# Layer 1, token tile 0: seven half-width products per pair of weight tiles, with a leaner attention start and a new instruction order

## The chip, the core and the metric

The kernel runs on one NeuronCore of a Trainium2 chip. Its engines are TensorE (PE in the profile; PEld is its weight load), VectorE (DVE), ScalarE (ACT), GpSimd (POOL) and SyncE (SP, which issues the loads here); 16 DMA engines move data. The metric is the device time of one execution in microseconds (us), as the median of several runs; lower is better.

## What is computed

Three stages follow each other: a linear attention with a decay per head, and two feed-forward layers, the first with ELU and the second with softplus between its two matrix products.

```python
def _attn_ref(q, k, v, lam):            # 2 x 8 heads x 768 tokens x 64
    ...
    for b in range(nb):                 # blocks of 64 tokens
        intra = np.einsum('bhic,bhjc->bhij', qb, kb) * Dmask[None]
        intra = np.einsum('bhij,bhjd->bhid', intra, vb)
        inter = np.einsum('bhid,bhde->bhie', qb * lam_pow[None], kv_state)
        out[:, :, sl] = intra + inter
        kv_state = lam_block[None, :, None, None] * kv_state + np.einsum('bhsd,bhse->bhde', kb_dec, vb)

x = attention, as 1536 tokens x 512
h = x @ w_in                            # 512 -> 2048
g = np.where(h > 0.0, h, np.exp(np.minimum(h, 0.0)) - 1.0)
x = g @ w_out                           # 2048 -> 512
h = x @ w_in2
g = np.maximum(h, 0.0) + np.log1p(np.exp(-np.abs(h)))
out = g @ w_out2
```

## The kernel before

**Number format.** Each large product is made of three matmuls in a rounded 32-bit format (`F32R`): a matrix is kept as a high part and a low part, and high x high, high x low and low x high are summed in PSUM (`product`, lines 335 to 337 for the first matrix of a layer; `m2_part`, line 386, for the second). Weights come from memory in 64-bit words, and four ScalarE and VectorE steps turn each tile of 128x512 into its two parts (lines 602 to 621 and the difference `minus`, line 527).

**Tiling.** The 1536 tokens are three tiles of 512 (tile 0, 1, 2). The 2048 inner features of a layer are 16 chunks of 128, in 8 pairs. Tile 0 is done plainly: one chunk takes 4 x 3 matmuls of 512 columns into one PSUM bank (`plain`, tile name `hps`). Tiles 1 and 2 together are done by a Strassen-Winograd scheme (`quick`): a pair of chunks for both tiles takes 7 products of 6 matmuls of 512 columns (tiles `pa`, `pb`, `pd`) in place of 8, with sums of weight tiles (`sum_ops`, tiles `s0`, `s1`, scratch `sumsw`) and sums of activations (`t1` to `t4`). Between the seven products ScalarE copies a bank out and VectorE adds to the copy, so that results share banks.

After a first product the activation function runs on ScalarE and VectorE (`act_ops`), which leaves the parts `g`; the second product then takes 12 matmuls for each chunk and tile into four banks `y`, and after several chunks VectorE adds those into `yacc` (line 1144). After layer 0, `split_ops` makes tile 0's new input parts out of `yacc`, and `second_sums` does so for tiles 1 and 2 with their sums.

**Attention.** The attention runs in 12 chunks of 128 tokens. `att_s` makes the scores (line 245), `att_sc` multiplies them by the decay mask on VectorE over 2 x 4 x 128 = 1024 columns (line 251), `att_x` makes the output (line 265), `att_state` the state's update (line 312, tile `stps`), `att_add` and `att_fade` keep the running state (lines 318 to 325), `att_prep` scales the queries by the decay powers `qpow` (line 222) and `att_prep_k` the keys (lines 228 and 230). `decays` fills the mask with 8 scans of 128 columns on VectorE, and `powers` fills `qpow` with 4 more.

**Order.** The program is written out by a planner in `build`: every step is an `Op` with a key (its due time), costs per engine (`MM3`, `SB_V` and others) and what it depends on, and `schedule` issues the ops engine by engine as its own clock says. `PLAN` lists the first products: `one` is a plain chunk of tile 0, `fast` a pair for tiles 1 and 2. In layer 1 four `one` are followed by two `fast`, four times. The order on every engine is then fixed. SP issues all loads, in the order of `FIRST_LOADS` first.

## Time and profile before

| | us |
|---|---|
| median of 3 runs | 556.19 (556.12 to 557.3) |
| the profiled execution | 555.85 |
| its span | 554.1 |
| first scores start on TensorE | 4.83 |
| last matmul starts | 549.90 |

The profiled execution's own time is 1.75 us more than its span and 0.34 us less than the median. A line of the profile gives the source line, the engine, the operation, the tile written and the tiles read, the shape, how often, the busy time and the mean length of one in ns. A length is from an instruction's start to its end; where instructions of one engine follow each other without a gap, the next starts before the last has ended, so the distance between two starts (called pitch here) is shorter than the length.

### The profile page before, as it was taken

Reading aid. Unit: us, or ns where it says so; the run is one execution under the profiler, and the core shown is the slowest. Engines: PE = TensorE matmul, PEld = TensorE weight load, DVE = VectorE, ACT = ScalarE, POOL = GpSimd, SP = SyncE. Lnnn points to the kernel's source line nnn. Section 1 sums busy time; section 2 is a strip of 40 time slices with the busy share of each in tenths; the row PEclk is TensorE's granted clock in tenths of the full one; section 3 lists DMA queues with packets and bytes.
Section 4 is the critical chain, followed back from the end, with each engine's and each line's share of the span. In section 5 each row is a group of like instructions: output and inputs, shape, how many; then the busy total and the mean of one; then the engine's idle time right before and its main releaser. Section 6 shows DMA issues by size and latency. Waiting matters only on the chain.

```text
span 554.1 us, 8536 instructions
## 1 busy us (share of the span) xinstructions
PE 541.4 (98%) x3215; PEld 447.4 (81%) x3215; DVE 492.4 (89%) x876; ACT 404.0 (73%) x758; POOL 2.2 (0%) x8
## 2 busy tenths in 40 slices
PE   7789999999999999999999999999999999999997
PEld 6677788888888888888888888888888888888885
DVE  7899999999489899657999999999999999986973
ACT  4677897768398487547877589979996779856820
POOL 0000000000000000000000000000000000000000
PEclk9999999999999999999999999999999999999999
DMA  8967443011024224201322101212231212000023
GB/s 325 397 227 272 155 152 112 2 38 55 23 77 151 77 76 148 81 1 38 103 71 94 38 1 38 77 38 77 76 101 52 77 39 76 1 0 2 1 99 129
DMA packets 14585, 49.84 MB, mean 90 GB/s; under 512 B 1744, under 2 KB 1744, under 8 KB 14544
## 3 DMA queue, kind: packets, MB, share of 16 engines
q1 hardware_dynamic: 14544, 49.30, 25.9%
q8 instruction: 25, 0.41, 0.3%
q14 instruction: 16, 0.13, 0.1%
HBM read 46.14 MB, written 3.15 MB: 89 GB/s over the span
## 4 chain that ended last, share of the span: by engine, by line
PE 90%; DMA 6%; DVE 1%; ACT 1%; SPq 0%; issue 0%; ACTq 0%
PE y L386 47%; PE pa L335 5%; PE pa L337 5%; PE pa L336 5%; PE hps L335 5%; PE hps L337 5%; PE hps L336 5%; DMA raw<-w 4%; PE pd L335 3%; PE pd L337 3%; PE pd L336 3%; DMA qk<-attqk 1%; PE pb L337 1%; PE pb L335 1%; PE pb L336 1%; DMA kv<-attkv 1%
## 5 line engine op out<-in xcount | busy, mean ns | idle before, releaser
L386 PE MATMUL y<-g,woh 128*128 128x512 f32 x384 | 118.4, 390 | 0.0
L386 PE MATMUL y<-woh,g 128*128 128x512 f32 x384 | 118.2, 389 | 0.0
L840 ACT ACTIVATE g<-v 128x512 fp32r<-128x512 f32 x96 | 60.3, 628 | 53.8 <-PE y L386 53.2
L527 DVE TENSOR_TENSOR g<-v,g 128x512 fp32r<-128x512 f32 x96 | 65.4, 685 | 21.4 <-ACT g L840 21.2
L386 PEld LDWEIGHTS y<-woh,g 128*128 128x128 f32 x384 | 72.1, 188 | 15.0
L386 PEld LDWEIGHTS y<-g,woh 128*128 128x128 f32 x384 | 71.9, 188 | 15.0 <-issue 0.2
L386 PE MATMUL y<-g,wol 128*128 128x512 f32 x192 | 74.7, 389 | 0.0
L386 PE MATMUL y<-wol,g 128*128 128x512 f32 x192 | 74.7, 389 | 0.0
L1144 DVE TENSOR_TENSOR yacc<-y,yacc 128x512 f32<-128x512 f32 x68 | 44.1, 684 | 7.2 <-PE y L386 7.2
L335 PE MATMUL hps<-xh,wih 128*128 128x512 f32 x128 | 50.3, 393 | 0.0
L336 PE MATMUL hps<-xl,wih 128*128 128x512 f32 x128 | 49.8, 389 | 0.0
L337 PE MATMUL hps<-xh,wil 128*128 128x512 f32 x128 | 49.8, 389 | 0.0
L602 ACT ACTIVATE r<-raw 128x512 f32<-128x512 f32 x64 | 42.6, 665 | 8.7 <-DMA raw<-w 4.1
L616 DVE CUSTOM_DVE_ANT_0 r<-r,c 128x1024 uint16<-128x1024 uint16 x64 | 43.8, 684 | 2.9 <-ACT c L606 2.5
L606 ACT ACTIVATE c<-raw 128x512 uint32<-128x512 uint32 x64 | 42.4, 662 | 0.7 <-DVE r L616 0.7
L386 PEld LDWEIGHTS y<-g,wol 128*128 128x128 f32 x192 | 36.0, 188 | 7.6
L386 PEld LDWEIGHTS y<-wol,g 128*128 128x128 f32 x192 | 36.0, 188 | 7.4
L821 DVE SCALAR_TENSOR_TENSOR u<-u,e 128x512 f32<-128x512 f32 x48 | 32.7, 683 | 3.2 <-ACT v L817 3.2
L527 DVE TENSOR_TENSOR v<-v,u 128x512 f32<-128x512 f32 x48 | 32.7, 684 | 0.2
L396 ACT ACTIVATE v<-v 128x512 f32<-128x512 f32 x48 | 29.9, 625 | 0.6
L396 ACT ACTIVATE e<-e 128x512 f32<-128x512 f32 x48 | 30.0, 625 | 0.4
L812 ACT ACTIVATE u<-e 128x512 f32<-128x512 f32 x48 | 29.8, 621 | 0.2
(174 smaller groups left out, 1084.6 us busy)
## 6 DMA issues: line engine op xcount, KB each, us to landing
raw<-w SPq DMA_DIRECT2D x64, 512.0 KB, 3.7
qk<-attqk SPq DMA_DIRECT2D x8, 512.0 KB, 7.2
kv<-attkv SPq DMA_DIRECT2D x8, 512.0 KB, 5.9
out<-yacc SPq DMA_DIRECT2D x12, 256.0 KB, 2.1
early<-attqk SPq DMA_DIRECT2D x2, 512.0 KB, 10.0
early<-attkv SPq DMA_DIRECT2D x2, 512.0 KB, 10.1
earlykv<-attkv SPq DMA_DIRECT2D x2, 512.0 KB, 11.2
earlyqk<-attqk SPq DMA_DIRECT2D x2, 512.0 KB, 10.4
```

The lines of the kernel that those rows point to most:

```text
L335: T.matmul(ps, wh[:, wo[i]], xa[i], start=(start and i == 0), stop=False, skip_group_check=True)
L336: T.matmul(ps, wh[:, wo[i]], xb[i], start=False, stop=False, skip_group_check=True)
L337: T.matmul(ps, wl[:, wo[i]], xa[i], start=False, stop=(stop and i == n - 1), skip_group_check=True)
L386: T.matmul(yps[m], a, b, start=(begins(key) and i == 0), stop=(ends(key) and i == 2))
L396: A.activation(out=o, in_=a, func=AF.Exp, scale=-1.0)
L527: engines[e].tensor_tensor(out=o, in0=a, in1=b, op=ALU.subtract)
L602: A.activation(out=r, in_=high.bitcast(F32), func=AF.Prelu, scale=2.0 ** -112, alpha=-2.0 ** 32)
L606: A.activation(out=box["c"], in_=box["low"], func=AF.Copy, scale=2.0 ** -29)
L616: V.tensor_tensor(out=ri, in0=ri, in1=box["c"], op=ALU.add)
L821: V.scalar_tensor_tensor(out=u, in0=u, scalar=-1.0, in1=box["e"], op0=ALU.add, op1=ALU.subtract)
L840: A.activation(out=g[:, 0], in_=box["v"], func=AF.Copy)
L1144: V.tensor_tensor(out=y, in0=yps[m], in1=y, op=ALU.add)
```

## The change

1. **Layer 1, tile 0.** The first four chunks (pairs 0 and 1) stay plain. Pairs 2 to 7 are done by the seven-product scheme over the tile's two halves of 256 tokens (`slim`; banks `za`, `zb`, `zd`). It takes the weight sums that tiles 1 and 2 use anyhow (`made_sums`). `zero_sums` replaces `split_ops` and makes the activation sums `z1`, `z2`, `z4` and, in place of a part of the input, a third. The plain product is no longer cut in four for the layer's first chunk.
2. **Attention.** The scores are packed so that the mask multiply covers 768 columns; the mask takes 4 + 8 scans of 64 columns; `qpow` comes from 8 small matmuls (`powers`) and one ScalarE copy. In `att_x` the second pairs of heads are split in two matmuls, with a `T.drain()` ahead of the last group. Fades go to GpSimd but for the first of them, as does the first chunk's key scaling.
3. **Start.** The small table `lam_t` is loaded from ScalarE's queue, and the first load of queries and keys is cut in two.
4. **Order.** New planner constants, a table `NUDGE` that shifts the keys of 52 ops, four shared scratch tiles (`e0` to `e3`), 12 activation buffers in place of 9, and 3 weight slots in place of 6 late in layer 1, whose room the `z` tiles take.

```diff
+NUDGE = {
+    338: -0.7, 340: -0.4, 344: 0.2, 353: 0.0, 356: 0.9, 360: -5.0, 362: 1.4, 364: 3.1, 373: 0.3, 384: -4.1, 387:
...
+SECOND = [
+    ("one", (0, 1, 2, 3)), ("fast", (0, 1)), ("slim", (2,)), ("fast", (2, 3)), ("slim", (3, 4)), ("fast", (4, 5)),
+    ("slim", (5, 6)), ("fast", (6,)), ("slim", (7,)), ("fast", (7,)),
+]
+UNITS = {2: (2,), 3: (3, 4), 5: (5, 6, 7)}
...
-    for b in range(4):
-        p += [("one", 1, c) for c in range(4 * b, 4 * b + 4)]
-        p += [("fast", 1, q) for q in (2 * b, 2 * b + 1)]
+    for kind, qs in SECOND:
+        p += [(kind, 1, q) for q in qs]
...
-        return n if n < 8 else 2 + (n - 8) % 6
+        return n if n < 8 else 2 + (n - 8) % 6 if n < NF + 4 else 5 + (n - NF - 4) % 3
...
     def setup():
-        nc.sync.dma_start(out=lam_t, in_=lamc)
+        A.dma_start(out=lam_t, in_=lamc)
...
-    def powers():
+    def powers(ps):
         for p in range(NPAIR):
-            V.tensor_tensor_scan(
-                out=qpow[:, p, :], data0=lam_t[:, H + p:H + p + 1].to_broadcast([P, P]), data1=zero,
-                initial=1.0, op0=ALU.mult, op1=ALU.add,
-            )
+            for e in range(2):
+                w = lam_t[:, H + NPAIR + 2 * p + e:H + NPAIR + 2 * p + e + 1].to_broadcast([P, 64])
+                x = dmask[:, e, p % 2, 0:2] if p < 2 else dmask[:, e, p % 2, 0::2]
+                T.matmul(
+                    ps[64 * e:64 * e + 64, P * p:P * p + P].rearrange("q (a i) -> q a i", a=2), w, x,
+                    start=True, stop=True, skip_group_check=True)
+
+    def powers_out(ps):
+        A.activation(out=qpow.rearrange("q a i -> q (a i)"), in_=ps, func=AF.Copy)
...
-        nc.sync.dma_start(out=qk, in_=attqk[g])
+        if g:
+            nc.sync.dma_start(out=qk, in_=attqk[g])
+        else:
+            for c in (slice(0, HALF), slice(HALF, DM)):
+                nc.sync.dma_start(out=qk[:, :, c], in_=attqk[g].rearrange("p (a i) -> p a i", a=2)[:, :, c])
...
-        sc[g] = ap2.tile([P, 2, NPAIR, P], F32, tag="sc", name="sc")
+        sc[g] = ap2.tile([P, 2, 384], F32, tag="sc", name="sc")
         V.tensor_tensor(
-            out=sc[g], in0=sps[g].rearrange("p e (a i) -> p e a i", a=NPAIR), in1=dmask, op=ALU.mult)
+            out=sc[g], in0=sps[g][:, :, :384], in1=dmask.rearrange("q e j a i -> q e (j a i)"), op=ALU.mult)
...
         for p, e in heads[0]:
-            intra(p, e, rows[e], 0, 64)
-        for p, e in heads[0]:
-            intra(p, e, slice(0, P), 64, 64)
+            intra(p, e, rows[e], 0, first_half(p))
+        for p, e in heads[0] + heads[1]:
+            intra(p, e, slice(0, P), 64, second_half(p))
+        if between:
+            between()
+        T.drain()
         for p, e in heads[1]:
-            intra(p, e, slice(0, P), 0, P)
+            intra(p, e, rows[1 - e], 0, first_half(p))
...
+            self.key += NUDGE.get(self.n, 0.0)
...
+    SLIM = 0.72
-    PILE, HELD, QUEUE, PACK = 2.9, 7.9, 3, 0.8
+    PILE, HELD, QUEUE, PACK = 2.9, 3.9, 1, 0.8
-    F_ON = {"G": (0.62, True), "V": (0.415, True)}
+    F_ON = {"G": (0.62, True)}
...
+        def slim(p):
...
+            p1 = pe(0, "a", lambda: (*halves[fa], c0), lambda: x(0, one), True, [need(fa), first[0]], bank_free)
+            k1 = copy_op("a", keys[0], one, pos[3] - 1.0, [p1])
+            p2 = pe(1, "b", lambda: (*halves[fa], c1), lambda: x(1, one), True, [need(fa), first[1]], bank_free)
+            a11 = add_op(keys[0], one, "b", pos[4] - 1.0, [p2, k1], lambda: give_bank(box["b"]))
+            p5 = pe(2, "d", lambda: W(0, c0), lambda: xt(1), True, [s12, t[1]], bank_free)
+            k5 = copy_op("d", keys[1], two, pos[4] - 1.0, [p5])
+            p6 = pe(3, "a", lambda: W(0, c1), lambda: xt(2), False, [k1, s12, t[2]])
+            k2 = copy_op("a", keys[0], two, pos[5] - 1.0, [p6, k1])
+            p3 = pe(4, "d", lambda: W(1, c0), lambda: x(1, two), False, [k5, s34, first[2]])
+            a12 = add_op(keys[0], two, "d", pos[6] - 1.0, [p3, k2], lambda: give_bank(box["d"]))
+            p7 = pe(5, "a", lambda: W(1, c1), lambda: xt(3), False, [k2, s34, t[3]])
+            a22 = add_op(keys[1], two, "a", pos[6] - 1.0, [p7, k5])
+            p4 = pe(6, "a", lambda: (*halves[fb], c1), lambda: xt(4), False, [a22, need(fb), t[4]])
+            k4 = copy_op("a", keys[1], one, nom["m2", keys[1]] - 3.0, [p4, k5], lambda: give_bank(box["a"]))
...
+        def zero_sums():
...
+            f1 = sub(pos[2], yy(0, one), yy(0, two), yy(0, one), [k11, k12, closed[0]])
+            f3 = sub(pos[2], yy(0, two), yy(1, two), yy(0, two), [f1, k12, k22])
+            f2 = sub(pos[3], yy(1, two), yy(1, two), yy(0, one), [f1, f3])
+            f4 = sub(pos[6], yy(1, one), yy(1, one), yy(1, two), [f2, k21])
```

Over the whole program the counts of instructions go from 384 to 240 matmuls of 512 columns into `hps`, and from none to 252 of 256 columns into `za`, `zb` and `zd`.

How the instructions stand is shown at three places. The first is VectorE at the attention's first chunks, from the first masked scores (`sc`) on; `xl` is the low part of the output, `state` and `faded` the running state. Before:

```order
L251 TENSOR_TENSOR sc<-aps_104,dmask 128x1024
L190 SCALAR_TENSOR_TENSOR qpow<-lam_t,zero 128x128 x4
L303 TENSOR_TENSOR xl_223<-aps_104,xh_222 128x4x128
L318 COPY state<-stps 128x256
L251 TENSOR_TENSOR sc<-aps_108,dmask 128x1024
L325 TENSOR_TENSOR faded<-state,qpow 128x256
L222 TENSOR_TENSOR qk<-qk,qpow 128x512
L251 TENSOR_TENSOR sc<-aps_104,dmask 128x1024
```

After:

```order
L325 TENSOR_TENSOR sc<-aps_107,dmask 128x768
L380 TENSOR_TENSOR xl_247<-aps_107,xh_246 128x4x128
L325 TENSOR_TENSOR sc<-aps_111,dmask 128x768
L279 TENSOR_TENSOR qk<-qk,qpow 128x512
L325 TENSOR_TENSOR sc<-aps_107,dmask 128x768
L395 COPY state<-stps 128x256
L279 TENSOR_TENSOR qk<-qk,qpow 128x512
L402 TENSOR_TENSOR faded<-state,qpow 128x256
```

The four scans for `qpow` are gone, the masked scores are narrower, and the state's first copy stands behind the third masked scores.

The second place is TensorE late in layer 1, where the sixth of the seven products hands its bank to the last one. Before, in a `fast` pair (tiles 1 and 2), with second products `y` between the two:

```order
L335 MATMUL pa<-t3h,s1h 128x512
L336 MATMUL pa<-t3l,s1h 128x512
L337 MATMUL pa<-t3h,s1l 128x512
L386 MATMUL y_4996<-woh_4435,g_5062 128x512 x2
L386 MATMUL y_4996<-wol_4463,g_5062 128x512
L386 MATMUL y_5004<-woh_4435,g_5062 128x512 x2
L386 MATMUL y_5004<-wol_4463,g_5062 128x512
L335 MATMUL pa<-t4h,wih_4637 128x512
```

After, in the last `slim` pair (pair 7 of tile 0):

```order
L412 MATMUL za<-xh_3146,s1h 128x256
L413 MATMUL za<-xl_3147,s1h 128x256
L414 MATMUL za<-xh_3146,s1l 128x256
L412 MATMUL za<-z4h,wih_5379 128x256
L413 MATMUL za<-z4l,wih_5379 128x256
L414 MATMUL za<-z4h,wil_5400 128x256
```

There nothing stands between the two products of that pair; in the other five `slim` pairs 6 to 36 matmuls `y` do.

The third place is SP's queue at the start. Before:

```order
L151 DMA lam_t<-lamc 128x12
L207 DMA qk<-attqk 128x1024
L217 DMA kv<-attkv 128x1024
L207 DMA qk<-attqk 128x1024
L217 DMA kv<-attkv 128x1024
```

After:

```order
L264 DMA qk<-attqk 128x2x256 x2
L274 DMA kv<-attkv 128x1024
L261 DMA qk<-attqk 128x1024
L274 DMA kv<-attkv 128x1024
L261 DMA qk<-attqk 128x1024
```

The table's load has left this queue, and the first load stands in two halves.

## Rows read from the trace of the kernel before

**Rows 1.** The page: busy time and share by engine, VectorE by slices, chain by engine.

```profile
PE 541.4 (98%) x3215; PEld 447.4 (81%) x3215; DVE 492.4 (89%) x876; ACT 404.0 (73%) x758; POOL 2.2 (0%) x8
...
DVE  7899999999489899657999999999999999986973
...
PE 90%; DMA 6%; DVE 1%; ACT 1%; SPq 0%; issue 0%; ACTq 0%
```

**Rows 2.** Busy time by stretch: length, then each engine's busy us and count.

```profile
core 0: us, PE busy (x) PEld busy (x) DVE busy (x) ACT busy (x) POOL busy (x), PEclk, DMA share, GB/s
5.00:25.00 20.00, 14.71 (x424) 12.55 (x424) 16.80 (x31) 12.51 (x41) 0.00 (x0) 1.00 1.02 397
25.00:51.00 26.00, 23.54 (x476) 19.28 (x476) 25.12 (x43) 18.94 (x45) 1.25 (x2) 1.00 0.74 271
...
300.00:500.00 200.00, 200.00 (x884) 165.55 (x883) 196.12 (x347) 163.97 (x302) 0.00 (x0) 1.00 0.15 48
500.00:550.30 50.30, 50.29 (x222) 41.29 (x221) 33.79 (x53) 24.04 (x41) 0.00 (x0) 1.00 0.13 46
```

**Rows 3.** Timeline of TensorE at 316 us: start, length, line, tiles, count.

```profile
316.19 0.39 PE L335 MATMUL pa<-xh,wih 128*128 128x512 f32 x1
316.42 0.39 PE L336 MATMUL pa<-xl,wih 128*128 128x512 f32 x1
```

**Rows 4.** Weight-load groups (count, busy us, mean ns); timeline of 256-column matmuls at the start.

```profile
L335 PEld LDWEIGHTS pa<-xh,wih 128*128 128x128 f32 x32 | 6.0, 188 | 1.2
...
L165 PEld LDWEIGHTS aps<-zr 128*128 128x128 f32 x4 | 1.0, 332 | 0.0
...
3.63 0.41 PE L165 MATMUL aps<-zr 128*128 128x256 f32 x1
3.85 1.05 PE L168 MATMUL warm<-zr 128*128 128x256 f32 x3
```

**Rows 5.** Waits of TensorE up to 52 us: us in total, times, longest.

```profile
PE aps L245 <- DMA qk<-attqk: 1.6, 2, 1.4
...
PE aps L265 <- DVE sc L251: 1.4, 1, 1.4
PE aps L245 <- DVE xl L303: 1.1, 2, 0.7
...
PE aps L265 <- DVE qk L222: 1.1, 2, 0.8
PE aps L265 <- DVE early L222: 0.8, 1, 0.8
```

**Rows 6.** Timeline of VectorE at 26 us, for its pitch by width.

```profile
26.45 0.68 DVE L303 TENSOR_TENSOR xl<-aps,xh 128x512 fp32r<-128x512 f32 x1
27.05 1.21 DVE L251 TENSOR_TENSOR sc<-aps,dmask 128x1024 f32<-128x1024 f32 x1
28.18 0.68 DVE L222 TENSOR_TENSOR earlyqk<-earlyqk,qpow 128x512 f32<-128x512 f32 x1
```

**Rows 7.** Groups by line and shape: scans for the powers, fades on both engines.

```profile
L190 DVE TENSOR_TENSOR_SCAN qpow<-lam_t,zero 128x128 f32<-128x128 f32 x4 | 1.4, 400 | 0.0
...
L325 POOL TENSOR_TENSOR faded<-state,qpow 128x256 f32<-128x256 f32 x2 | 1.2, 623 | 47.7 <-DVE state L320 47.7
```

**Rows 8.** Timeline of SP's first two loads.

```profile
0.80 0.38 SPq L151 DMA_DIRECT2D lam_t<-lamc  x1
1.24 0.42 SPq L207 DMA_DIRECT2D qk<-attqk  x1
```

**Rows 9.** Groups of small attention matmuls: count, busy us, mean ns of one.

```profile
L265 PE MATMUL aps<-sc,early 128*64 128x128 f32 x16 | 1.2, 273 | 0.0
...
L312 PE MATMUL stps<-early 128*64 128x64 f32 x32 | 1.1, 222 | 0.0
```

**Rows 10.** Groups of 256 columns: a copy of ScalarE and an operation of VectorE from PSUM.

```profile
L303 DVE TENSOR_TENSOR xl2b<-aps,xh2b 128x256 fp32r<-128x256 f32 x4 | 1.7, 420 | 1.3 <-ACT x L299 1.3
...
L295 ACT ACTIVATE xh2b<-aps 128x256 fp32r<-128x256 f32 x4 | 1.5, 382 | 0.5 <-PE aps L265 0.5
```

More of the change, by code (lines that the diff above doesn't have):

```diff
@@ L161, in setup @@
             T.matmul(ps[:, :P], zero, zero, start=True, stop=True)
[L163 to L166 removed]
+        for n, times in ((256, 5), (384, 2)):
             for i in range(times):
@@ L353, in body @@
             queue.append((layer, 0, c))
+        elif kind == "slim":
+            queue += [(layer, 0, 2 * q + i) for q in UNITS.get(c, ()) for i in range(2)]
         elif c % 2:
@@ L757, in take_v, with take_temp, copied @@
             return k, new_v(k)
-        eu = [0, 1]
+        vbuf = {}
+        temps = list(range(4))
+        def take_temp():
+            k = temps.pop(0)
+            return k, late["tp"].tile([P, TT], F32, tag=f"e{k}", name=f"e{k}")
+        def copied(key, e, src):
+            vbuf[key] = take_v(key)
+            if e == "A":
+                A.activation(out=vbuf[key][1], in_=src, func=AF.Copy)
+            else:
+                V.tensor_copy(vbuf[key][1], src)
         m1_seq, m2_seq = [], []
@@ L829, in act_ops @@
                 gate = v_gate(key)
-                o = Op({"A": SCALAR}, k, s1, after + [closed[0]], lambda: eu and gate())
+                o = Op({"A": SCALAR}, k, s1, after + [closed[0]], lambda: len(temps) > 1 and (not bank or gate()))
                 o = Op({"A": SCALAR}, k, s2, [o])
                 o = Either(PLUS_ONE, k, s3, [o])
-                o4 = Op({"A": SCALAR}, k, s4, [o])
-                o5 = Op({"V": SB_V}, k, s5, [o4])
-                o6 = Either(SOFT, k, s6, [o5], end=lambda: eu.append(box["i"]))
@@ L1166, in unit_ops @@
                 ysplit[t] = mine
[L1168 to L1186 removed]
+        tz, zdone = {}, {}
@@ L1275, in build @@
             if kind == "one":
-                o = plain(layer, 0, c, layer == 1 and c == 0)
+                o = plain(layer, 0, c)
                 xuse[0] = [o]
                 keys_done.add((layer, 0, c))
+                if (layer, c) == (1, 3):
+                    last_part[0]()
+            elif kind == "slim":
+                slim(c)
+                keys_done.update((layer, 0, 2 * c + i) for i in range(2))
             else:
@@ L1294, in body @@
     NV = 9
+    vfree = set(range(NV))
     W_LO = {"V": SB_V}
```

432 lines of the change are left out of this document (290 added, 142 removed), and 5 rows, old and new, of the table NUDGE.

## Prediction

> **What bounds the kernel now.** I read the page first: TensorE is busy for 98% of the span and stands on 90% of the chain that ended last [rows 1]. Then the stretches: from 51 us to the end of the products TensorE leaves next to nothing idle, and all of its lost time lies ahead of that, 5.3 us between 5 and 25 us and 2.5 us between 25 and 51 us [rows 2]. So a saved matmul after 51 us is saved time, as long as TensorE's inputs keep up. That they do is no matter of course: between 300 and 500 us VectorE is busy for 196.1 of 200 us, and only after 500 us does it have room, 33.8 of 50.3 us [rows 2]. Late in the program TensorE and VectorE are nearly level. At the start TensorE waits for VectorE in four groups that add up to 4.4 us (masked scores, low parts, scaled queries twice) and for a load, 1.6 us [rows 5]; VectorE is busy for 25.1 of 26 us between 25 and 51 us, and the DMA engines are full between 5 and 25 us [rows 2].
>
> **Strassen on tile 0: matmuls.** Removed are 144 matmuls of 512 columns (12 chunks of 12), added 252 of 256 columns (6 pairs, 7 products, 6 each). A 512-column matmul follows the one before it after 0.227 us (316.19 to 316.42; the starts of one chunk give 0.2267) [rows 3]. [...] The removed work is 144 x 0.2267 = 32.6 us, the added 252 x 0.120 = 30.2 us: **2.4 us less**; in proportion 4.1 us less. [...]
>
> The weight load is what could spoil this. One lasts 188 ns in the steady stretch [rows 4], longer than 120 ns. [...] If the load ran at a pace of its own and didn't quicken with the array, 188 ns would be the bound: 252 x 0.188 = 47.4 us, 14.7 us more than what is removed. I give that little, and take 0.130 us as the upper end (it breaks even).
>
> **Strassen on tile 0: the other engines.** VectorE gets 18 additions of 256 columns (three per pair), four sums and four more low parts of 512 columns, and four more copies that ScalarE did. Its pitch is 0.60 us for 512 columns (26.45 to 27.05) [rows 6]; for 256 I take 0.335 us, from the length of 0.420 [rows 10] less the 0.08 us by which 0.68 exceeds 0.60. That is 18 x 0.335 + 12 x 0.60 = 13.2 us. The room from 300 us on is 3.9 + 16.5 = 20.4 us [rows 2], and TensorE takes back 2.4 of it, so 4.8 us stay: VectorE has to be busy for about 98% to the end. It was so for 200 us without TensorE waiting; that the room after 500 us can be used follows from the order of the work (the final run of second products shrinks from 135 to 102 matmuls, so first products stretch further into it). ScalarE gets 24 copies of 256 columns and four high parts, about 10 us, and has 36 us free in 300 to 500 us [rows 2]: nothing.
>
> **Waits inside the seven products.** A product now lasts 0.72 us, not 1.36. When ScalarE has copied out the fourth product's bank, the sixth may go, and only the fifth lies between unless second products do; so it is with the third product, the fourth and the fifth. The loop is the end of a matmul (0.39 - 0.23 = 0.16 us after its stream) [rows 3], a copy of 0.38 us [rows 10] and two hand-overs that I put at 0.08 us each: 0.70 against 0.72 us. It fits if ScalarE is idle; it is busy for 82% [rows 2], so some 0.2 us is lost. By the order three pairs (4, 6, 7) have no second product there, with two such hand-overs each: 6 x 0.2 = 1.2 us; some copies will find ScalarE free, so 1.0 us. In pair 7 nothing at all lies between the sixth and the last product, while VectorE adds: 0.16 + 0.42 [rows 10] + 0.16 = 0.74 us. Together **1.7 us more**; between 0 and 4, since each VectorE step may queue.
>
> **The start and the attention.** The loads go out 0.44 us earlier (0.80 against 1.24) [rows 8], and since the DMA engines are full then, all early landings move with them: 0.4 us less. [...] VectorE loses the scans for the powers (1.4 us) and fades (seven of eight on GpSimd, two were: five x 0.33) [rows 7], and 256 of 1024 columns of twelve masked scores: a pitch of 1.13 us (27.05 to 28.18) [rows 6] against 0.60 for 512 is about 1.04 ns a column, so 12 x 0.27 = 3.2 us. Its new small steps cost what the narrower mask scans save. Of 6.3 us I credit TensorE with 2.4 us, over half of the 4.4 us of waits [rows 5], as several of these will wait for a load or a copy instead; bounds 0 and 4.4. A fade on GpSimd takes 0.62 us [rows 7], off TensorE's path. [...]
>
> On TensorE each chunk now empties the array once: a small matmul lasts 222 ns where 32 of them take 1.1 us, 34 ns each [rows 9], so 0.19 us is exposed. Two groups of 64 columns in place of one of 128 save next to nothing (0.6 us for eight of 128 columns [rows 9]). 12 x 0.13 = 1.6 us, part of it where TensorE waits anyway: 1.0 us more; bounds 0 and 2.4. The attention's sum is -0.4 - 2.4 + 1.0 = **1.8 us less**, between 4.8 less and 2 more.
>
> **The sum.** 555.85 (the profiled execution, 554.1 in its span) - 2.4 + 1.7 - 1.8 = 553.35 us. The median of the runs is 0.34 us above the profiled one: 553.7 us. What 0.2% means, 1.1 us, is about what a measurement of this kernel tells from no change.
>
> **Rivals.**
> 1. *Nothing gets in the way.* [...] Chance 0.18.
> 2. *The seven products don't pay.* Either 256 columns take 0.130 us (0 and the 1.7 of waits), or they take 0.120 and the waits 4 us (-2.4 + 4 = 1.6): 555.85 + 1.7 - 1.8 + 0.34 = 556.1 us. For it: three pairs go from product to product without second products. Against it: VectorE and ScalarE keep up with such hand-overs now. Chance 0.16.
> 3. *VectorE becomes the bound of layer 1 (slower).* Place: from 300 us on. If the 16.5 us after 500 us can't be filled, because VectorE waits there for TensorE's last products as it does now, 13.2 us meet 3.9 us of room: 9.3 us late, 555.85 + 9.3 - 1.8 + 0.34 = 563.7 us. It decides from the point where VectorE idles more than the 4.8 us left. The attention's relief of VectorE and the longer run of first products speak against it, the 98% for it. Chance 0.10.
> 4. *The weight load bounds 256 columns (slower).* The 188 ns of a load set the pitch, +14.7 in place of -2.4: 553.7 + 17.1 = 570.8 us. Against it the start's 0.22 us with loads of 332 ns [rows 4]. [...] Chance 0.04 for both.
>
> **The numbers.** The forecast, 553.7 us, gets 0.52; its own spread is 551.5 to 555.0. Faster by over 1.1 us are the forecast and rival 1: 0.70. Within 1.1 us is rival 2: 0.16. Slower: rivals 3 and 4, 0.14. A range of 549.8 to 557.5 us leaves out rivals 3 and 4 and the best of rival 1, about 2 in 10.
>
> **What would show it.** Right: `za` matmuls 0.12 us apart; TensorE without gaps from about 48 us on but for some tenths at pairs 4, 6 and 7; VectorE at 97 to 99% from 300 to 520 us and idle for less than 6 us behind that; the first product of layer 0 starting 1 to 3 us earlier. Wrong: `za` 0.19 us apart (rival 4); TensorE waiting for `g` or for VectorE's additions by several us in layer 1 (rival 3); waits at the first scores as long as now, with the drains on top.

## The result, and the profile after

The changed kernel takes **559.19 us** (median of 6 runs, 558.01 to 560.16) against 556.12 us of the kernel before beside it: ratio 1.0056, 95% interval 1.0037 to 1.0075. It is slower by 3 us, where the prediction said 553.7 us, faster, and 557.5 us at the most. The profiled execution lies at the median (559.15 us, span 557.4 us).

The page after, its busy line and the chain's shares by engine, as in [rows 1]:

```profile
PE 543.0 (97%) x3435; PEld 453.2 (81%) x3435; DVE 502.5 (90%) x907; ACT 413.5 (74%) x775; POOL 7.8 (1%) x14
...
PE 87%; DVE 7%; ACT 2%; issue 1%; DMA 1%; SPq 0%; DVEq 0%; ACTq 0%
```

TensorE is busy 1.6 us longer although columns were saved, and "issue", time in which an engine waited for nothing that the profile shows, is on the chain. The stretches, columns as in [rows 2]:

```profile
5.00:25.00 20.00, 14.80 (x400) 12.66 (x404) 12.38 (x24) 9.99 (x31) 3.09 (x4) 0.95 1.02 404
25.00:51.00 26.00, 24.22 (x514) 19.94 (x508) 22.75 (x38) 19.11 (x48) 2.93 (x4) 0.97 0.67 235
300.00:500.00 200.00, 199.20 (x974) 168.18 (x973) 195.89 (x351) 164.45 (x307) 0.00 (x0) 1.00 0.16 51
500.00:553.50 53.50, 52.98 (x254) 44.37 (x252) 47.72 (x83) 37.53 (x67) 0.00 (x0) 1.00 0.14 52
```

From 300 us on it is nearly as forecast: VectorE is busy for 98% up to 500 us and for 89% behind that, and TensorE lacks only 1.3 us. The start is not: between 5 and 25 us VectorE is busy for 4.4 us less than before (12.38 against 16.80), and TensorE has gained nothing from it. The first product of layer 0 starts at 30.63 us (26.14 before), the 100th matmul of 512 columns at 75.29 us (72.12 before): **the start loses 3.2 us**. From the 1200th on to the last, layer 1 for the most part, it is 229.06 us against 228.66: **0.4 us more**.

What TensorE waits for from 5 us to the first product, in the kernel before and then in the changed one (us in total, times, longest):

```profile
PE aps L245 <- DMA qk<-attqk: 1.4, 1, 1.4
PE stps L312 <- ACT earlykv L228: 1.4, 1, 1.4
PE aps L265 <- DVE sc L251: 1.4, 1, 1.4
PE aps L265 <- DVE early L222: 0.8, 1, 0.8
PE aps L245 <- DVE xl L303: 0.4, 1, 0.4
```

```profile
PE stps L389 <- issue: 2.5, 1, 2.5
PE aps L308 <- DMA qk<-attqk: 1.8, 1, 1.8
PE aps L339 <- issue: 1.2, 1, 1.2
PE aps L339 <- DMA kv<-attkv: 0.3, 1, 0.3
PE aps L339 <- DVE state L395: 0.3, 1, 0.3
```

The waits for VectorE fell from 2.6 to 0.3 us. In their place stand 3.7 us of "issue". The longer of these stops, in TensorE's timeline (start, length, line, tiles, count of records, idle time ahead; a record is the trace's entry for one instruction), and the kernel before at the same place:

```profile
18.80 0.56 PE L389 MATMUL stps<-early 128*64 128x64 f32 x11
21.87 0.39 PE L389 MATMUL stps<-early 128*64 128x64 f32 x5 [2.51 <-issue]
22.18 0.96 PE L308 MATMUL aps<-early 64*64 64x128 f32 x32
```

```profile
18.73 0.34 PE L312 MATMUL stps<-earlykv 128*64 128x64 f32 x4
20.44 0.57 PE L312 MATMUL stps<-earlykv 128*64 128x64 f32 x12 [1.38 <-ACT earlykv L228]
```

The stop falls into the middle of a group, after 11 of 16 records: no tile and no engine is waited for there. In the kernel before the view names ScalarE, but its last scaling of that tile had ended at 19.66 us, 0.8 us ahead of 20.44. What arrives in these microseconds beside the data is a packet of instructions; that they are TensorE's is read from their count (27 packets in the whole trace for its 6926 records, one for each 256). The DMA view by queue of 19.2 to 20.4 us (packets, MB, share of 16 engines):

```profile
q1 hardware_dynamic: 125, 0.45, 94.8%
q8 instruction: 1, 0.02, 5.3%
```

After the stop, the granted clock is 0.50 for 3.4 us (length, busy us of PE, PEld, DVE, ACT, POOL, granted clock, DMA share, GB/s):

```profile
19.00:22.80 3.80, 1.29 (x43) 1.09 (x42) 1.83 (x3) 3.19 (x10) 1.00 (x1) 1.00 1.02 406
22.90:26.30 3.40, 3.40 (x69) 3.05 (x60) 3.10 (x5) 0.00 (x0) 0.73 (x1) 0.50 1.02 412
26.30:51.00 24.70, 22.92 (x487) 18.75 (x486) 21.45 (x37) 19.11 (x48) 2.63 (x3) 1.00 0.65 225
```

TensorE had stood still for 2.5 of the 3.8 us ahead. In the 3.4 us at a granted clock of 0.50, 16 outer products took 1.12 us (at 23.07 us; 0.69 at 36.01 us). If everything took twice as long there, 1.7 us were lost: an estimate from the 0.50, and the upper end. All six runs of the changed kernel had a mean granted clock of 0.991 to 0.997; the profile of before has 1.00. A lowered clock is not new with the change, though: of 85 executions of the kernel before beside the experiments, 57 had 0.999 or 1.000 and 28 had 0.996 to 0.998, these 0.9 us slower in the medians.

### The profile page after: what moved, and what is told of

Its sections match the earlier page's. It is cut to its first block, busy times and chain, and to the rows that moved or that the text cites. A ratio compares the mean times of both kernels' runs of the same rounds, so it can differ in the third digit from the quotient of the medians.

```text
span 557.4 us, 9041 instructions
## 1 busy us (share of the span) xinstructions
PE 543.0 (97%) x3435; PEld 453.2 (81%) x3435; DVE 502.5 (90%) x907; ACT 413.5 (74%) x775; POOL 7.8 (1%) x14
## 4 chain that ended last, share of the span: by engine, by line
PE 87%; DVE 7%; ACT 2%; issue 1%; DMA 1%; SPq 0%; DVEq 0%; ACTq 0%
PE y L465 44%; PE pa L413 5%; PE pa L412 5%; PE pa L414 5%; PE hps L412 3%; PE hps L413 3%; PE hps L414 3%; PE aps L339 3%; PE pd L413 2%; PE pd L414 2%; PE pd L412 2%; DMA qk<-attqk 1%; PE pb L413 1%; PE pb L414 1%; PE pb L412 1%
## 5 line engine op out<-in xcount | busy, mean ns | idle before, releaser
L475 ACT ACTIVATE e<-e 128x512 f32<-128x512 f32 x72 | 45.0, 626 | 0.8
L967 ACT ACTIVATE e<-e 128x512 f32<-128x512 f32 x48 | 30.0, 626 | 9.8 <-DVE e L964 9.5
L610 DVE TENSOR_TENSOR e<-e,e 128x512 f32<-128x512 f32 x48 | 32.6, 683 | 2.3 <-ACT e L967 2.1
L964 DVE SCALAR_TENSOR_TENSOR e<-e,e 128x512 f32<-128x512 f32 x48 | 32.7, 683 | 1.3 <-ACT e L958 1.3
L412 PE MATMUL hps<-xh,wih 128*128 128x512 f32 x80 | 31.7, 396 | 0.0
L413 PE MATMUL hps<-xl,wih 128*128 128x512 f32 x80 | 31.2, 390 | 0.0
L414 PE MATMUL hps<-xh,wil 128*128 128x512 f32 x80 | 31.1, 389 | 0.0
L958 ACT ACTIVATE e<-e 128x512 f32<-128x512 f32 x48 | 30.0, 625 | 0.5
```

The costliest lines, as they stand in the source:

```text
L412: T.matmul(ps, wh[:, wo[i]], xa[i], start=(start and i == 0), stop=False, skip_group_check=True)
L413: T.matmul(ps, wh[:, wo[i]], xb[i], start=False, stop=False, skip_group_check=True)
L414: T.matmul(ps, wl[:, wo[i]], xa[i], start=False, stop=(stop and i == n - 1), skip_group_check=True)
L475: A.activation(out=o, in_=a, func=AF.Exp, scale=-1.0)
L610: engines[e].tensor_tensor(out=o, in0=a, in1=b, op=ALU.subtract)
L964: V.scalar_tensor_tensor(out=e, in0=box["u"], scalar=-1.0, in1=e, op0=ALU.add, op1=ALU.subtract)
```

## The experiments

All eighteen runs, against 556.1 to 556.3 us for the kernel before beside them (555.88 beside e17 and e18):

| run | median us | ratio, 95% interval |
|---|---|---|
| whole first load (e1) | 560.51 | 1.0063 to 1.0111 |
| old attention in the changed kernel (e2) | 560.23 | 1.0059 to 1.0106 |
| new attention in the kernel before (e3) | 564.90 | 1.0138 to 1.0187 |
| narrow warming matmuls (e4) | 563.68 | 1.0114 to 1.0156 |
| Strassen alone (e5) | 563.45 | 1.0111 to 1.0154 |
| before, array emptied (e6) | 558.43 | 1.0026 to 1.0065 |
| before, outputs split (e7) | 557.16 | 1.0011 to 1.0042 |
| before, outputs merged (e8) | 557.25 | 1.0000 to 1.0030 |
| changed, loads as before (e9) | 559.58 | 1.0043 to 1.0070 |
| before, wide outer products (e10) | 557.27 | 1.0010 to 1.0032 |
| before, GpSimd fades (e11) | 561.10 | 1.0077 to 1.0105 |
| before, powers on TensorE (e12) | 556.31 | 0.9993 to 1.0022 |
| before, loads paced (e13) | 568.86 | 1.0212 to 1.0249 |
| changed, loads paced (e14) | 569.38 | 1.0212 to 1.0250 |
| changed, fades on VectorE too (e15) | 566.23 | 1.0163 to 1.0191 |
| changed, paced to three (e16) | 562.31 | 1.0079 to 1.0138 |
| changed, old layer 1 (e17) | 559.96 | 1.0042 to 1.0098 |
| before, late loads paced (e18) | 559.88 | 1.0043 to 1.0097 |

Theory A: the attention costs the time. Rival B: the loads do. Rival C: the products of layer 1 do.

### Loads: one edit undone, then both (e1, e9)

```diff
-        if g:
-            nc.sync.dma_start(out=qk, in_=attqk[g])
-        else:
-            for c in (slice(0, HALF), slice(HALF, DM)):
-                nc.sync.dma_start(out=qk[:, :, c], in_=attqk[g].rearrange("p (a i) -> p a i", a=2)[:, :, c])
+        nc.sync.dma_start(out=qk, in_=attqk[g])
```

> The changed kernel with one edit undone: the first load of queries and keys goes out as one transfer again, not as two halves. Theory A (the new attention costs the time: more instructions on TensorE, the array emptied in every chunk, and a stop of 2.5 us at 19.4 us while its next instructions are fetched): the later loads go out 0.5 us earlier, and the time falls by 0.3 to 0.8 us, to about 558.6 us; the stop stays, with its length between 1.5 and 2.6 us. Rival B (the two halves cost it: every load behind them is 0.4 to 0.6 us late and the waits grow with that): falls by 2.5 us or more, below 556.7 us. Rival C (the new order and the seven products of layer 1 cost it): no change, 559.2 us.

Slower than the changed kernel by 1.3 us: none of the three. VectorE's first mask scan, in the changed kernel and in this one, shows what changed:

```profile
2.54 0.84 DVE L213 TENSOR_TENSOR_SCAN dmask<-lam_t,ids 128x64 f32<-128x64 f32 x4 [0.40 <-DMA lam_t<-lamc]
```

```profile
4.52 0.84 DVE L213 TENSOR_TENSOR_SCAN dmask<-lam_t,ids 128x64 f32<-128x64 f32 x4 [2.38 <-DMA lam_t<-lamc]
```

The data of the first large load start 0.4 us sooner here (1.82 against 2.23 us), and the small table, on ScalarE's queue, is waited for 2 us longer; halving the first load had kept that off. So the next run put the table back ahead on SyncE's queue, with the whole load:

> The changed kernel with the loads issued as before: the small table first and on SyncE's queue, the first load in one piece. In the run with the whole load alone the small table, on ScalarE's queue, landed 2 us later (4.52 against 2.54 us), behind the first large loads, and the masks with it; here it goes ahead of them. If the two halves cost anything by themselves (all later loads 0.4 to 0.6 us late), this is 0.3 to 0.8 us faster than the changed kernel, about 558.6 us. If the start is paced by the instructions of TensorE, as theory A says, the border ahead of the 705th record is reached earlier and waits longer: within 0.4 us of the changed kernel's 559.2.

559.58 us, the changed kernel's time; the place of the long stop, its length (2.58 us) and the stretch at a granted clock of 0.50 (22.6 to 26.1 us) are the same. Rival B, with its 2.5 us and more, is out. That the time agrees is partly luck, though: in this trace the 100th matmul starts 1.0 us earlier than in the changed kernel's (74.28 us), and one wait in layer 0, which neither the changed kernel nor the kernel before has, takes that back:

```profile
PE pa L408 <- DVE v L1127: 1.0, 1, 1.0
```

Whether the loads cost the start up to 1 us stays open.

### The two halves of the change apart (e2, e5, e3, e17)

> The changed kernel with the whole attention of the kernel before (scores in 1024 columns, decay powers by scans on VectorE, no emptying of the array, first load in one piece, the small table first on SyncE's queue); tile 0 of layer 1 by Strassen and the order of the weights stay as changed. Theory A: layer 1 gains the 0.6 us that its trace shows (2.4 of columns less 1.8 of waits), so 0.3 to 1.2 us faster than before: about 555.4 us. Rival B also lands there (the halves are gone too) and is told apart by the run with the whole load. Rival C: 558 to 559 us, as slow as the changed kernel.

> The attention, its planner's costs and the order of its loads are the kernel before's, word for word on TensorE's queue for the first 150 steps; tile 0 of layer 1 goes by Strassen, with the changed order of the weights and the list of shifts. What the run with the old attention but the new planner's costs left mixed is apart here. Theory A (the attention costs the time, layer 1 gains 2.4 of columns less 1.8 of waits): 0.3 to 1.0 us faster than before, 555.6 us, with the first product of layer 0 at 26 us. Rival C (the seven products of layer 1 cost more than they save): 556.5 us or more although the first product starts as early as before.

> The kernel before with the new attention alone: scores in 768 columns, the decay powers on TensorE, the array emptied once per chunk; loads, the order of the loads and layer 1 are as before. Theory A: slower than before by 2 to 4 us, about 559 us, with the array-emptying steps 0.25 us each at twelve places and a stop of TensorE where its instructions are fetched. Rival B (the loads): 0 to 0.5 us slower, 556.4 us. Rival C: faster by about the 1.8 us that the prediction gave to the attention, 554.3 us.

e2 kept the new planner's costs, e5 took the old costs, keys and margins, e3 is the kernel before with the new functions. All three missed what theory A said, and none separates the halves: the planner orders the whole program anew. In e5 the start is that of before (first product at 26.23 us, 100th matmul at 72.74), and the stretch from the 1200th matmul on takes 5.5 us longer: 7.9 us lost, 2.4 saved in columns. Its longest waits from 300 us on:

```profile
PE y L409 <- ACT g L928: 1.8, 1, 1.8
PE pa L356 <- DVE v L1067: 1.0, 1, 1.0
PE za L356 <- DVE v L1140: 0.8, 1, 0.8
```

So Strassen on tile 0 without the changed planner's costs is 7 us slower: rival C holds for that order. In the changed kernel's order the same stretch loses 2.8 us and saves 2.4. For layer 1, e17 is the clean comparison, as TensorE's first 150 steps are those of the changed kernel:

> The changed kernel's attention, loads and planner's costs (the first 150 steps of TensorE are the same) with layer 1 as in the kernel before: tile 0 by plain products of 512 columns, the old order of the weights, no list of shifts. If layer 1 by Strassen costs 0.4 us in sum, as the traces read (2.4 saved in columns, 2.8 lost in stops), this is 0.4 us faster than the changed kernel: 558.5 to 559.0 us, and the attention alone makes 2.6 us. If Strassen gains the 0.7 us of the prediction, it is 559.9 us.

559.96 us. The median falls on the second branch, but the interval (2.3 to 5.4 us above the kernel before) holds both, and the changed kernel's ratio of 1.0056. So layer 1 does not make the 3 us; a difference of up to about 2 us stays open in the times, and the traces give 0.4 us. The start makes the loss. Whether that is the new attention or the order that the new costs give it is not shown, since e17 has both, and the changed loads too. e2 has the old attention in the new order, and its 100th matmul starts at 75.2 us, as late as the changed kernel's. Its five runs at a clock of 1.00 took 559.9 to 560.4 us, so a lowered clock is no part of its loss. What TensorE waits for there, up to 76 us, is VectorE in the main, 7.3 us in all (4.4 us up to 52 us in the kernel before [rows 5]):

```profile
PE aps L266 <- DVE xl L324: 2.9, 3, 1.4
PE aps L286 <- DVE qk L243: 2.4, 3, 1.2
PE aps L286 <- DVE sc L272: 1.4, 1, 1.4
...
PE aps L266 <- issue: 0.6, 1, 0.6
```

### What TensorE stops for (e4)

```diff
-        for n, times in ((256, 5), (384, 2)):
+        for n, times in ((64, 32),):
```

> The changed kernel with its warming matmuls cut narrower: 32 of 64 columns in place of five of 256 and two of 384, the same 2048 columns, but 25 matmuls (50 instructions on TensorE) more ahead of the attention. If the stop at 19.4 us (after 11 of the 16 records of chunk 3's outer products) is TensorE running out of fetched instructions, it moves ahead by 25 records, to about the 18th of the 32 records of chunk 3's scores, and the second one (after the 9th record of chunk 4's outputs) to the first records of the step ahead of it; their lengths may differ, since the transfers then in flight are others, and the time stays within 1.5 us of 559.2. If a tile of data or another engine makes it, both stay where they are.

Both stops moved as the count said; the first one:

```profile
22.90 0.77 PE L308 MATMUL aps<-early 64*64 64x128 f32 x18
24.02 0.46 PE L308 MATMUL aps<-early 64*64 64x64 f32 x14 [0.35 <-issue]
```

The first stands behind the 18th of 32 records of the scores, where it was behind the 11th of 16 of the outer products; the second lies ahead of the first record of the step forecast, with a wait for VectorE on top. The time, 4.5 us above the changed kernel's where I had said 1.5 at the most, is not usable: 64 columns took as long as 256 do in [rows 4] (32 matmuls in 7.0 us, 0.22 us each), and everything starts 5.0 us later.

With TensorE's records (weight loads, matmuls, waits, drains) numbered from 0, all stops that the view puts down to "issue", and the kernel before's of 1.4 us, lie ahead of records 449, 705 and 961, in whichever kernel (e13, e14 and e18 have none). These places, called borders here, are 256 records apart, and one transfer of 16 KB, by division 64 bytes for each, comes in between (27 transfers, 0.44 MB, for the changed kernel's 6926 records, 24 for the 6277 of e8). The table, counted from the traces ("reaches" is the end of the record before, "goes on" the start of record 705, which overlaps it where there is no stop):

| kernel | passes 449 | next transfer | reaches 705 | goes on | stop |
|---|---|---|---|---|---|
| before | 14.73 | 18.10 to 19.21 | 19.07 | 20.44 | 1.4 |
| changed | 14.74 | 19.29 to 20.30 | 19.36 | 21.86 | 2.5 |
| outputs split (e7) | 14.22 | 17.92 to 18.99 | 18.64 | 20.48 | 1.8 |
| wide outer products (e10) | 16.47 | 19.65 to 20.76 | 21.31 | 22.11 | 0.8 |
| changed, paced to three (e16) | 16.82 | 18.70 to 19.63 | 22.47 | 22.25 | none |
| changed, paced (e14) | 19.79 | 20.45 to 21.38 | 25.38 | 25.16 | none |

In the table each transfer starts after TensorE has passed the border before it (in the kernel before, one at 34.40 us starts 1.1 us ahead of its border). While the DMA engines are full (a share of 1.02 between 5 and 25 us in the kernel before, the changed one and e10) it starts 3.2 to 4.5 us behind the border, in the table's first four rows, and takes 1.0 to 1.1 us. Where TensorE stops at a border, in these rows and at record 961 of the changed kernel, it goes on 1.2 to 1.6 us after the transfer's end. So 256 instructions took 5.6 to 7.1 us there (from record 449 to 705 in the table's first four rows), while 128 small matmuls of 34 ns [rows 9], a weight load for each, would be done in 4.4, an estimate from that row. Behind 50 us 256 instructions are 128 products of 0.227 us, 29 us by that pitch, and from 51 us on none of TensorE's waits is put down to "issue", in the kernel before or the changed one.

### Does the count or the work set the pace? (e7, e10, e8)

```diff
-        for p, e in heads[1]:
-            intra(p, e, slice(0, P), 0, P)
+        for i in (0, 64):
+            for p, e in heads[1]:
+                intra(p, e, slice(0, P), i, 64)
```

> The kernel before with the outputs of the last four heads in two matmuls of 64 columns each in place of one of 128: the same columns, nothing emptied, but 16 more of TensorE's records (weight loads and matmuls) in each chunk, 192 in all, as the changed kernel has. In six kernels TensorE stood still ahead of its 705th record, whatever work that was, and went on 1.2 to 1.6 us after the transfer of its next 256 instructions had ended; each such transfer starts only when TensorE has passed the border 256 records before. If that supply sets the pace up to 30 us, 16 records cost about 16/256 of 6 us, 0.37 us a chunk, so 1.5 to 2.5 us in the five or six early chunks, and less behind them. If only the work counts, 0.1 to 0.6 us.

0.9 us slower, under the range that the supply gave and above the work alone. The stop at record 705 is 1.8 us in place of 1.4, and at record 961, where the kernel before has none, there is one of 1.5 us:

```profile
20.48 0.67 PE L245 MATMUL aps<-early 64*64 64x128 f32 x20 [1.83 <-issue]
...
26.50 0.34 PE L265 MATMUL aps<-sc,earlykv 128*64 128x64 f32 x4 [1.48 <-issue]
```

The opposite, more work in as many instructions:

```diff
-                T.matmul(ps[r, D * p:D * p + D], a[2][:, o], a[3][:, o], start=True, stop=True, skip_group_check=True)
+                b = slice(P * p, P * p + P)
+                T.matmul(ps[r, b], a[2][:, o], a[3][:, b], start=True, stop=True, skip_group_check=True)
```

> The kernel before with the outer products of keys and values twice as wide (128 columns in place of 64): TensorE's number of instructions stays, its columns grow; the odd heads take the wrong half, so their part of the output is not the reference's. By its rows 32 records of this kind take 1.1 us, so a chunk costs 0.55 us more, 5.5 us over ten chunks, of which five lie ahead of the first product of layer 0. If the work sets the pace there, the first product moves from 26.1 to about 28.8 us and the time rises by 4.0 to 5.5 us. If the supply of instructions sets it, the first product moves by less than 1 us, the stops at the 705th and 961st record shrink by what is added, and the time rises by 2.5 to 3.7 us.

A chunk costs 0.40 us more (I had said 0.55), as a later chunk shows, before and here:

```profile
43.12 0.64 PE L312 MATMUL stps<-kv 128*64 128x64 f32 x16
```

```profile
45.63 1.04 PE L312 MATMUL stps<-kv 128*64 128x128 f32 x16
```

That is 4.0 us over ten chunks, and the kernel takes 1.2 us longer, less than either theory said. The traced execution is the slowest of the twelve (558.91 us), with a stretch of lowered granted clock from 7.5 to 10.9 us (0.91 in the mean of 5 to 25 us); in it the stop at record 705 is 0.8 us, with another of 0.6 at record 961. One trace tells little about half a microsecond of a stop: e5 has TensorE's steps of the kernel before up to there, and stops for 0.9 us at record 705, not 1.4. What the times show is that most of the added work does not arrive at the end, and that added instructions cost something without a column more. The third run took instructions away:

> The kernel before with the outputs of the first four heads in one matmul of 128 columns over all 128 keys in place of two of 64 (the masked scores there are zero): 16 records fewer on TensorE in each chunk, 192 fewer in all, the same columns. By the supply of instructions it is 1 to 2 us faster than before, about 554.7 us, and the stop at 19 us gets shorter or goes. If only the work counts, within 0.3 us of before.

No gain (557.25 us). The border is reached later with fewer instructions, so the next transfer starts later too (19.99 us), and a stop of 0.9 us stays. It doesn't confirm the theory: none of the three runs fell into the range that the supply of instructions gave, and that it sets the pace rests on the stops and their times alone. The runs of e8 part by the clock: four with a mean granted clock of 0.999 to 1.000 took 555.4 to 556.2 us, eight with 0.996 to 0.997 took 556.7 to 558.7, a difference of 2.0 us in the medians; how much of it is the clock and how much the idle time ahead of its fall is not separated.

### The parts of the new attention, one by one in the kernel before (e6, e12, e11, e15)

```diff
+        T.drain()
         for p, e in heads[1]:
```

> The kernel before with one thing added: TensorE's array is emptied once per chunk, ahead of the outputs of the last four heads, as the changed kernel does. The change's trace shows 0.26 us beyond a matmul's pitch at each of the twelve places. Theory A1 (each counts in full): 3.0 us slower than before, 559.2 us. Theory A2 (up to 30 us TensorE gets its instructions in blocks of 256, and a block's arrival sets the pace, whatever is done in between): only those in later chunks count, 1.0 to 1.8 us slower. The prediction's step: 1.0 us of 1.6.

2.1 us slower, between A1 and A2. The group with the drain, before and here:

```profile
35.48 1.17 PE L265 MATMUL aps<-sc,kv 64*64 64x64 f32 x24
```

```profile
37.23 1.48 PE L265 MATMUL aps<-sc,kv 64*64 64x64 f32 x24
```

0.31 us each, 3.7 us for twelve, of which 2.1 arrive at the end.

> The kernel before with the decay powers alone made on TensorE (eight matmuls, copied out by ScalarE) in place of four scans on VectorE, 1.36 us; loads and order as before. By the prediction's rate (2.4 of 6.3 us) this brings 0.5 us: 555.8 us. By the supply of instructions its 32 more records cost 32/256 of about 6 us, 0.7 us, less what the scans gave: 0 to 0.7 us slower.

0.2 us slower, not distinguishable from zero: the 1.4 us of scans taken off VectorE brought no more than the new matmuls cost.

> The kernel before with the changed kernel's choice for GpSimd: all fades but the first scale of queries go there, and the first key scaling too (the planner then sets some steps in another order). The prediction gave VectorE's relief 2.4 of 6.3 us; by that rate the 2.3 us that are moved here bring 0.9 us: 555.4 us. If the start is paced by the supply of instructions instead, relief of VectorE brings nothing, and GpSimd's longer fades (0.62 us and more against 0.41) lie on the path from chunk to chunk: 0 to 1.5 us slower than before.

```diff
-    F_ON = {"G": (0.62, True), "V": (0.415, True)}
+    F_ON = {"G": (0.62, True)}
```

(and the same for the first key scaling, with the queue length at which GpSimd takes work set to 1). 5.0 us slower, more than any theory said. TensorE's waits up to 60 us have the stops at two borders again:

```profile
PE stps L312 <- issue: 2.4, 1, 2.4
...
PE aps L265 <- issue: 1.3, 1, 1.3
```

and the granted clock is 0.50 from 23.3 to 30.2 us. So GpSimd looked like the culprit, and the reverse was tried in the changed kernel:

> The changed kernel with one choice of the planner undone: fades and key scaling may go to VectorE, ScalarE or GpSimd as before (the plan then puts all fades on VectorE and moves some steps of the attention). If GpSimd's fades cost the start, as in the kernel before (5.0 us), this is 2 to 4 us faster than the changed kernel: 555 to 557 us. If they do not, because the step that matters there was the order and not the engine, 558.5 to 562 us.

7 us slower than the changed kernel, the wrong way. Either choice, made in a plan whose costs were set for the other, moves steps of the attention (TensorE waits 2.3 us for low parts, 1.2 us for a state). The engine of the fades is not shown to be the cause; that the order decides several microseconds is.

### Is the backlog of loads what delays the instructions? (e13, e14, e16, e18)

```diff
+    def paced(x):
+        k = len(marks)
+        if 2 <= k < 14:
+            nc.sync.dma_start(out=pace[:, k:k + 1], in_=marks[k - 2][0:1, 1, 0:1])
+        marks.append(x)
...
+        paced(qk)
         nc.sync.dma_start(out=qk, in_=attqk[g])
```

> The kernel before with its early loads paced: ahead of each of the loads 3 to 14 of queries, keys and values SyncE issues a transfer of four bytes that waits until the load two before has landed, so that about two loads are in flight and not up to eight. If the instruction transfers wait behind the backlog of loads, they start 1 us or less after TensorE has passed a border (2.8 to 3.7 us now), and the stop of 1.4 us at the 705th record goes; the early data may come up to 1 us later each: 554.5 to 556.5 us. If the backlog is not what delays them, the stop stays at 1 to 1.5 us, and the time is that of before or, with later data, up to 3 us more.

> The changed kernel with the same pacing, two loads in flight. If the backlog delays the instructions, the stops of 2.5 and 1.2 us at the 705th and 961st record go or shrink by half, the granted clock may stay at 1.0, and the time falls by 1.5 to 4 us, to 555 to 557.5 us. If not, the stops stay and the time is 559 to 562 us.

> The changed kernel with the loads paced to three in flight in place of two: the DMA engines stay fuller and the data come earlier, the instructions wait for more. If the backlog sets the delay of the instructions, the delay lies between those of the changed kernel (3.5 to 4.6 us behind the first three borders) and of the run with two loads in flight; the time is 555.5 to 558.5 us. If not, 559 us as the changed kernel.

The mechanism was right and the times were not. With two loads in flight the transfer behind record 449 starts 0.4 us ahead of it to 0.7 us behind it (3.4 and 4.5 us behind without pacing), with three 1.9 us behind it. The stop at 705 is gone (in e16 one of 0.5 us stays at 961): in e14 and in e16 the group that was cut in two runs through:

```profile
24.87 0.69 PE L399 MATMUL stps<-early 128*64 128x64 f32 x16
```

```profile
21.96 0.69 PE L399 MATMUL stps<-early 128*64 128x64 f32 x16
```

But the DMA engines move 220 GB/s between 5 and 25 us in e14, not 404, and the data come late:

```profile
5.00:25.00 20.00, 13.64 (x324) 11.32 (x325) 8.76 (x17) 6.31 (x20) 1.66 (x2) 0.83 0.66 220
```

```profile
PE aps L318 <- DMA qk<-attqk: 5.1, 2, 4.4
```

> The kernel before with pacing (three loads in flight) only from the tenth load of queries, keys and values to the fifteenth, which are needed from 20 us on; the first nine go out as before. If the delay of the instructions behind the second border follows the backlog, it falls from 3.4 us to about 2, and the stop of 1.4 us at the 705th record goes without the data of the first chunks coming later: 554.5 to 556 us. If the paced loads come too late for their chunks, waits for them appear behind 20 us and the time is 556.5 to 560 us.

The second branch: record 705 is passed without a stop, but chunk 4's keys come late (TensorE waits 1.7 us for their scaling, 1.7 us for a scaled query). In all four runs the attention got its data too late when its loads were held back, and with the loads at the full rate the backlog delayed the instructions. None took the stops away without other waits in their place, so what the stops cost is not shown by a time. No version found beats the kernel before.

## Why the prediction was wrong

**Columns, 2.4 us less: right.** The 0.120 us of a 256-column matmul in that sum was my estimate; no row of the kernel before shows it. In the changed kernel's trace the 252 matmuls of 256 columns follow each other after 0.12 us, as here in pair 6, behind its stop:

```profile
492.44 0.38 PE L412 MATMUL za<-z4h,wih 128*128 128x256 f32 x1 [0.43 <-DVE v L1204]
492.67 0.28 PE L413 MATMUL za<-z4l,wih 128*128 128x256 f32 x1
492.79 0.28 PE L414 MATMUL za<-z4h,wil 128*128 128x256 f32 x1
```

Rival 4 (0.188 us) is out. **Waits inside the products, 1.7 us: right in size.** Three stops, 0.53 us at 485.7, 0.59 at 491.6 and 0.68 at 515.2 beyond the pitch, make 1.8 us; pairs 6 and 7 had them, not pair 4. The 0.08 us of a hand-over was an assumption: in pair 6 VectorE's addition ends at 492.39 us and the weight load that waits for it starts at 492.44. What I left out: behind each stop the weight load (0.19 us) starts only with its matmul at 492.44, and the next matmul comes after 0.23 us (at 492.67), not 0.12; and thousandths in many places, together 1.0 us. The sum for layer 1 is -2.4 + 2.8 = +0.4, not -0.7: rival 2's mechanism, in its milder half.

**VectorE's room: right.** 195.89 of 200 us, then 47.72 of 53.5: rival 3 is out in this order. e5 shows what it looks like in another.

**Loads 0.4 us earlier: wrong in sign.** I took the 0.80 us start of SyncE's queue for all loads and forgot that the halved load is two issues, 1.30 us together in the trace; the next four loads went out 0.4 to 0.6 us later, the five behind them 0.8 to 1.5 us. In the whole e9 shows no difference; up to 1 us at the start stays open.

**VectorE's relief, 2.4 us less: the step that failed.** The cause was right, the waits for VectorE fell by 2.3 us up to the first product, as the two lists in the section on the result show. I said that some would turn into waits for a load or a copy. Instead the stops for TensorE's own instructions, which I had no term for, grew by as much, from 1.4 to 3.7 us, and the upper bound of 0 for this step held only as long as nothing else became worse. The row that could have told it stood in the trace of before: a stop of 1.4 us that cut a group after 4 of 16 records, put down to an operation that had ended 0.8 us earlier. I named 6.0 of the 7.8 us that TensorE was idle up to 51 us; the stop lies in the 1.8 us that I left unnamed.

**The array emptied, 1.0 us more: half of what it is.** I had 0.13 us a chunk, which no run shows, though the length of a matmul had given 0.19, which makes 2.3 us for twelve; the change's trace shows 0.26 beyond the pitch and e6 0.31, with 2.1 us at the end. **Narrower outputs, "next to nothing": wrong.** The columns are the same, the instructions are 16 more per chunk; alone they cost 0.9 us (e7). **Powers on TensorE**: their 1.4 us of VectorE were in the relief, their matmuls had no term; e12 says that the exchange brings nothing.

**The clock: no term.** With it, the start adds up: from 5 us to the first product, stops +0.7 us (6.1 against 5.4 in the two lists), five drains of 0.26, together 1.3, the granted clock of 0.50 up to 1.7 (the estimate from above), the powers' matmuls 1.1 and a longer first score step 0.5 (1.53 against 1.07 us): up to 5.3, and 4.5 is measured. This says where TensorE's time went, not what each part would give back: after the stretch at 0.50 TensorE reached record 961 at 27.67 us and went on only at 28.91, 1.4 us after its transfer had ended, so without that stretch it might only have stood there longer. Of the 4.5 us, 1.3 come back by the 100th matmul: TensorE waits for 1.0 us in that stretch, for 2.0 in the kernel before.

So the sum's attention term was -1.8 with a bound of +2, and the start is +3.2. The rivals for "slower" were both in layer 1; none had the start as its place, and none the new order. The share of each part is not settled, nor that of the order (e2): drains 2.1, instructions 0.9 and powers 0.2 were measured in the kernel before, one at a time, and they don't add up to e3's 8.6.

I took 0.62 us for a fade on GpSimd. In the changed kernel's trace it takes 0.62 us at 15.42 us, with VectorE all but idle, and at 37.33 us, 0.73 us at 24.57 us, and 1.00 to 1.12 us in the four of seven places where an operation of VectorE like the scaling of `qk` by `qpow`, which reads two tiles outside PSUM, had started 0.04 to 0.17 us ahead of it. From the timelines of the two engines:

```profile
15.42 0.62 POOL L402 TENSOR_TENSOR faded<-state,qpow 128x256 f32<-128x256 f32 x1 [6.64 <-ACT early L285]
...
41.16 0.67 DVE L279 TENSOR_TENSOR qk<-qk,qpow 128x512 f32<-128x512 f32 x1
...
41.31 1.00 POOL L402 TENSOR_TENSOR faded<-state,qpow 128x256 f32<-128x256 f32 x1 [3.36 <-DVE state L397]
```

## What to carry to other kernels

In a stretch of many small matmuls under full DMA queues, count TensorE's instructions, not only its columns: here 4.0 us of added columns cost 1.2 us, and 192 added instructions with no column more 0.9 us. Where a stop cuts a group of equal matmuls in two, or its named releaser ended long before, look whether an instruction transfer ended shortly ahead of it (1.2 to 1.6 us here), and whether the stops lie 256 records apart. Relief of one engine is worth its waits only if the next limit lies further off; write that limit down with its own number before crediting the relief. Add up the waits that a trace names against the idle time that it shows: what is left over is a limit without a name.

## What the runs showed of the hardware

- TensorE's instructions came in transfers of 16 KB, one for each 256 records (27 for 6926 in the changed kernel). The one behind record 449 started 3.4 and 4.5 us after that border under full queues (kernel before and changed, DMA share 1.02), 1.9 us with three loads in flight (e16), 0.7 us after to 0.4 us ahead of it with two (e14, e13). Where TensorE stopped at a border, in the kernel before, the changed one, e7 and e10, it went on 1.2 to 1.6 us after the transfer's end.
- A small load on another queue was waited for 2 us longer (the scan behind it starts at 4.52 against 2.54 us) when the data of the first large load started 0.4 us sooner (e1).
- A matmul of 64 columns in the warming run (e4) took as long as one of 256 in the kernel before: 32 of them 7.0 us, 0.22 us each, against 0.22 us from 3.63 to 3.85 us.
- A drain of TensorE's array took 0.26 us (changed kernel) and 0.31 us (e6) between small matmuls. In a run of 256-column matmuls the first one behind a stop was followed after 0.23 us, the others after 0.12 us (changed kernel, 492.44 to 492.79 us).
